# Turning two blocks of memory V by DMA, splitting the last copy and the first half of Wo in a two-part kernel on one core

## The chip, the cores and the metric

The kernel runs on one core of a Trainium2 chip. The metric is device time in microseconds (us) from one execution of the whole program; the runs of one kernel are summed up by their median. A profile of one execution adds, for each engine, when every instruction ran and what it waited for. The engines are named as the profile names them: PE (TensorE), DVE (VectorE), ACT (ScalarE), POOL (GpSimd) and SP (SyncE, which only issues DMAs).

## What is computed

Two independent models run on two inputs, and their outputs stand side by side in the last dimension. Part A is a diagonal state-space layer, part B attention with a recurrent memory of 8 rows in front of every segment of 32 tokens:

```python
def _A_ref(x, Lambda_re, Lambda_im, B_re, B_im, C_re, C_im, log_dt, Dskip):
    ...
    for t in range(L):
        h = Lam_bar[None, :] * h + Bu[:, t, :]
        hs.append(h)
    hseq = jnp.stack(hs, 1)
    y = 2.0 * jnp.einsum('blp,dp->bld', hseq, Cmat).real + x * Dskip[None, None, :]
    return y

def _B_ref(x, mem0, Wq, Wk, Wv, Wo, seg_len):
    ...
    mem = mem0
    for s in range(n_seg):
        xs = x[:, s * seg_len:(s + 1) * seg_len, :].copy()
        h = jnp.concatenate([mem, xs], axis=1)
        q = jnp.einsum('btd,dhe->bhte', h, Wq)
        k = jnp.einsum('btd,dhe->bhte', h, Wk)
        v = jnp.einsum('btd,dhe->bhte', h, Wv)
        scores = jnp.einsum('bhqe,bhke->bhqk', q, k) * scale
        scores = jnp.where(mask[None, None], scores, -1000000000.0)
        p = _softmax(scores, axis=-1)
        o = jnp.einsum('bhqk,bhke->bhqe', p, v)
        o = jnp.einsum('bhte,hed->btd', o, Wo)
        mem = o[:, :M, :].copy()
        outs.append(o[:, M:, :])
    return jnp.concatenate(outs, axis=1)
a = _A_ref(...)
b = _B_ref(...)
return jnp.concatenate([a, b], axis=-1)
```

Part A has 2048 tokens, width 1024 and 1024 complex states; part B has 2048 tokens in 64 segments, width 1024, 32 heads of 128, and 8 memory rows that each segment hands to the next. Inputs and outputs are bfloat16.

## The kernel before

**Stages.** The program is unrolled and runs in four stages.

1. Projections of V for all tokens of part B (`v_x`, in units of four tiles of 128 tokens for one of 8 head blocks of 4 heads) woven into part A's first stage (`stage1`: B products, then the scan). V rows go to DRAM, one tensor `b_vx` for each head block (`self.vx[hb]`). This stage ends at about 344 us.
2. Part A's output products (`stage2`): 16 tiles of 128 tokens, each in two halves of 512 columns, so 32 steps i = 0 to 31 of 16 matmuls. Between the steps stand pieces of part B: the values of the memory rows are first guessed (`og`, `guess`) and then, at i = 24 to 27, the memory's V rows of head blocks 0 and 1 are made by `v_mem`. This stage ends at about 467 us.
3. The q and k projections (`proj`) woven into attention (`attention`, `att_front`, `att_back`) by head pair, 16 pairs of 11 units. Before head pair hp, `load_v` brings its V from DRAM into the tile `b_v`: the padding of partitions 99 to 127 (for the first two pairs only), the rows of `b_vx`, and the rows of `b_vt`. Within this stage, at unit n = 12, the first half of the output weights is loaded into `wo0` (printed as tile `t` in the profile), and `v_mem` runs for head blocks 2 to 7.
4. The output products (`outproj_first`, `outproj`, `check`, `out_last`); the last tile's columns are done in pieces of 512, 256 and 256, so that little is left after the last matmul.

At the end a flag chooses a general path, which is not taken with these inputs.

**Memory V.** `v_mem` (L557) multiplies the memory columns of `b_xe` with a head block's `b_wv` into a PSUM tile `psP`, one row for each value column and 71 columns for the memory rows, and copies that to `b_vm` (L565). The rows are then wanted with memory rows on the partitions. Head blocks 0 and 1 turn them with four PE transposes each (L581) into another `psP`, copy to a staging tile `b_vst` on DVE (L583), and store from there with SP: one DMA to `b_vx` (L585) and three to `b_vt` (`store_t`, L555). Head blocks 2 to 7 turn them by DMA (L566 to L577): `b_vm` is cleared behind column 71, written to DRAM as `b_vmt`, read back by a transposing DMA into `b_vst`, and stored from there, all issued by SP. `v_mem` is a generator: each `yield` hands over to the next step of the loop around it.

**Order.** A scheduler orders each engine's instructions by when it takes them to be ready. PE and SP are held to the program's order in stage 1, SP also in stage 2; in stages 3 and 4 both are free, but for single instructions that are pinned behind all that was written before them on their engine (`keep_in_program_order`). Two of the three DMAs of `load_v` are pinned in this way: the padding and the rows of `b_vx`. A queue issues its DMAs strictly in its order, and one that waits holds up those behind it. The landing of DMAs from SP and ACT is told by eight semaphores, which the DMAs take in turn.

**The last piece.** `out_last` (L815) copies its three pieces with DVE, ACT, DVE (`k.copy("vsv"[i], ...)`, L823) and stores each with SP (L824). The three psP buffers and the one output tile `b_ost` are shared by the pieces.

**The queue of ACT in stage 2.** ACT issues the sixteen copies of `a_ot` (part A's output tile, two buffers) to DRAM (L345).

The loop around `v_mem` in stage 2 is at L1111 to L1129, the load of `wo0` at L1149.

## Time and profile before

| what | value |
|---|---|
| median of 3 runs | 1238.36 us (1238.14 to 1238.47) |
| profiled execution, whole / span | 1238.14 us / 1236.4 us |
| DMA, share of 16 engines over the span | q1 (SP) 48.4%, q10 (ACT) 6.1% |
| DMA moved | 174.20 MB, mean 141 GB/s |
| copies b_vm<-psP on DVE | 8, 455 ns each |
| copies b_vst<-psP on DVE in v_mem | 2, 410 ns each, the first at 445.9 us |
| transposing DMAs b_vst<-b_vmt on SP | 6, 565.6 to 901.1 us |
| load of wo0 (4096 KB) | issued at 510.35 us, 0.37 us of the queue |
| last copy b_ost<-psP on DVE | 128x256, 425 ns, at 1232.26 us |

The span runs from the first to the last instruction; the whole time has some 1.7 us around it. Busy time is the time in which an engine's instructions run; idle time in brackets stands before an instruction, with what ended it. "PEld" is the loading of weights, which overlaps PE. DMA issues stand at their queue's engine (SPq, ACTq), with the time that the issue took in the queue, not the time of the transfer.

### The profile page before, as it was taken

How to read it: one execution, taken by the hardware profiler on the slowest of the kernel's cores; microseconds unless marked ns; L12 is line 12 of the kernel's file. 1: busy time of each engine (PE TensorE's matmuls, PEld its weight loads, DVE VectorE, ACT ScalarE, POOL GpSimd, SP SyncE). 2: the span in 40 equal slices, each digit the busy share in tenths (PEclk: the TensorE clock that was granted, in tenths of full speed). 3: DMA queues.
4: the chain of work that ended last, by engine and by line, in shares of the span. 5: the costliest groups of instructions: out<-in, count | busy, mean ns of one | idle time of the engine just before them, and what ended most of it. 6: DMA issues, size and time to landing. Idle time of an engine off the chain costs nothing.

```text
span 1236.4 us, 19973 instructions
## 1 busy us (share of the span) xinstructions
PE 1226.7 (99%) x8104; PEld 655.0 (53%) x8174; DVE 680.7 (55%) x1270; ACT 266.6 (22%) x694; POOL 271.8 (22%) x437
## 2 busy tenths in 40 slices
PE   9999999999999999999999999999999999999998
PEld 4444444444455555556666656555665554445444
DVE  4799999998711124666666666666666641001000
ACT  4444444443310000211112211111221110000000
POOL 4111232112322321322222222323222320000000
PEclk9999999999999999999999999999999999999999
DMA  9943455562798834855464645546574279507000
GB/s 246 246 148 93 126 141 143 154 172 89 232 306 258 248 120 95 234 125 139 96 154 109 154 108 135 127 91 132 115 151 97 62 208 234 113 17 154 18 17 27
DMA packets 321268, 174.20 MB, mean 141 GB/s; under 512 B 145882, under 2 KB 308876, under 8 KB 321172
## 3 DMA queue, kind: packets, MB, share of 16 engines
q1 hardware_dynamic: 299076, 145.33, 48.4%
q10 hardware_dynamic: 21072, 24.38, 6.1%
q0 software_dynamic: 1024, 3.17, 0.7%
q8 instruction: 65, 1.06, 0.4%
q14 instruction: 31, 0.25, 0.1%
HBM read 84.42 MB, written 53.96 MB: 112 GB/s over the span
## 4 chain that ended last, share of the span: by engine, by line
PE 94%; DVE 4%; issue 1%; DMA 0%; ACT 0%; SPq 0%; DVEq 0%
PE psP L69 80%; PE psU L69 7%; PE psS L69 3%; PE psO L69 2%; PE psR L69 1%; DVE a_pr L284 1%; DVE a_pr L274 1%; DVE a_pr L279 1%; DMA b_xr<-in_B_x_dram 0%; DVE a_n L299 0%; DVE a_h L302 0%; DVE a_fr L232 0%; DVE a_tabh L243 0%; DVE a_tabh L240 0%; ACT a_g L285 0%
## 5 line engine op out<-in xcount | busy, mean ns | idle before, releaser
L69 PE MATMUL psP<-b_xe,b_wk 128*128 128x480 bf16 (+1 forms) x1280 | 247.5, 343 | 0.0
L69 PE MATMUL psP<-b_xe,b_wq 128*128 128x480 bf16 (+1 forms) x1280 | 247.5, 343 | 0.0
L69 PE MATMUL psP<-b_wv,b_xe 128*128 128x512 bf16 (+2 forms) x1027 | 223.0, 372 | 1.3 <-ACT b_xe L94 0.2
L689 POOL TENSOR_TENSOR b_m<-b_e,maskB 99x396 bf16<-99x396 bf16 (+1 forms) x160 | 134.7, 842 | 335.4 <-ACT b_e L688 335.4
L688 ACT ACTIVATE b_e<-psS 99x396 bf16<-99x396 f32 (+3 forms) x208 | 91.5, 442 | 530.4 <-PE psS L69 530.4
L69 PEld LDWEIGHTS <-b_wk 128*128 128x128 bf16 x1280 | 119.2, 98 | 94.2
L69 PEld LDWEIGHTS <-b_wq 128*128 128x128 bf16 x1280 | 118.5, 98 | 87.7
L69 PEld LDWEIGHTS <-b_xe 128*128 128x128 bf16 x1056 | 101.9, 98 | 119.1 <-ACT b_xe L94 0.4
L96 DVE CAST b_k<-psP 128x480 bf16<-128x480 f32 (+1 forms) x192 | 97.3, 528 | 100.0 <-PE psP L69 100.0
L96 DVE CAST b_q<-psP 128x480 bf16<-128x480 f32 (+1 forms) x192 | 97.3, 529 | 92.2 <-PE psP L69 90.9
L69 PEld LDWEIGHTS <-b_ol 128*128 128x128 bf16 x864 | 84.3, 98 | 94.4
L69 PE MATMUL psU<-a_xT,a_bt 128*128 128x512 bf16 x500 | 114.1, 379 | 0.6
L69 PE MATMUL psP<-t,a_hl 128*128 128x512 bf16 x497 | 112.3, 379 | 0.8
L96 DVE CAST b_ost<-psP 128x512 bf16<-128x512 f32 (+1 forms) x17 | 11.5, 676 | 177.6 <-PE psP L69 176.6
L69 PE MATMUL psP<-wo,b_ol 128*128 128x512 bf16 (+1 forms) x440 | 91.9, 364 | 0.4
L69 PE MATMUL psP<-t,b_ol 128*128 128x512 bf16 x408 | 91.7, 379 | 0.4
L94 ACT ACTIVATE b_vst<-psP 128x512 bf16<-128x512 f32 x126 | 72.5, 589 | 76.0 <-PE psP L69 69.9
L289 POOL TENSOR_SCALAR a_tt<-a_pr,a_tabf 128x1 f32<-128x1 f32 x48 | 34.7, 723 | 245.4 <-DVE a_pr L284 245.4
L706 DVE TENSOR_TENSOR b_ob<-psO,b_accR 99x384 bf16<-99x384 f32 x160 | 86.0, 554 | 2.9 <-DVE b_accR L705 0.4
L69 PEld LDWEIGHTS <-a_bt 128*128 128x128 bf16 x512 | 49.8, 98 | 59.5
L69 PEld LDWEIGHTS <-a_hl 128*128 128x128 bf16 x512 | 49.1, 98 | 56.7
L274 DVE TENSOR_TENSOR a_pr<-psU,a_tabf 128x2048 f32<-128x2048 f32 x32 | 73.1, 2283 | 9.2 <-PE psU L69 9.1
(203 smaller groups left out, 968.5 us busy)
## 6 DMA issues: line engine op xcount, KB each, us to landing
b_v<-b_vx SPq DMA_DIRECT2D x16, 1122.0 KB
b_wv<-in_B_Wv_dram SPq DMA_DIRECT2D x16, 1024.0 KB
b_vx<-b_vst ACTq DMA_DIRECT2D x24, 544.0 KB
b_on<-b_ob SPq DMA_DIRECT2D x15, 720.0 KB
a_hs<-a_h SPq DMA_DIRECT2D x32, 256.0 KB
b_wog<-in_B_Wo_dram SPq DMA_DIRECT2D x4, 2048.0 KB
b_wq<-in_B_Wq_dram SPq DMA_DIRECT2D x16, 512.0 KB
b_wk<-in_B_Wk_dram SPq DMA_DIRECT2D x16, 512.0 KB
```

The costliest lines, as they stand in the source:

```text
L69: r = f(*a, **kw)
L94: self.S.activation(out, in_, ACT.Copy)
L96: self.V.tensor_copy(out, in_)
L274: V.tensor_tensor(pr[:], u[:].unsqueeze(1).to_broadcast([128, 2, 2, TB]), view(t3, [[TB + 1, 2], [TB + 1, 2], [1, TB]]), ALU.mult)
L279: V.tensor_tensor(w, w, pr[:, :, 1, :], ALU.add)
L284: V.tensor_tensor_scan(w[:, j, :], rb, w[:, j, :], 0.0 if ini is None else ini[:, j:j + 1], ALU.mult, ALU.add)
L289: G.tensor_scalar(tt[:, j:j + 1], w[:, j, TB - 1:TB], t3[:, 1, TB:TB + 1], None, ALU.mult)
L688: k.S.activation(e[:, a:b, :, 0:n], s[0:GW, a:b, :, 0:n], ACT.Exp, scale=float(E) ** -0.5, accum_out=self.accE[0:GW, j:j + 1])
L689: k.G.tensor_tensor(mv[:, a:b, :, 0:n], e[:, a:b, :, 0:n], mask[0:GW, :, 0:n].unsqueeze(2).to_broadcast([GW, b - a, 2, n]), ALU.mult)
L706: V.tensor_tensor(self.ob[:, b0:b0 + n, :], o[0:GW, 0:n, 0:E], r.unsqueeze(2).to_broadcast([GW, n, E]), ALU.mult)
```

## The change

1. `v_mem` turns the rows of all head blocks by DMA; the PE transposes, their PSUM tile and the copy out of it are gone. For head blocks 0 and 1 the six DMAs (write of `b_vmt`, transpose, store to `b_vx`, three stores to `b_vt`) are issued by ACT, for the others by SP as before. `store_t` takes the queue as an argument.
2. In stage 2, `v_mem` of head block 1 starts at i = 27 in place of 26, and the generators are stepped at i = 24 to 29 in place of 24 to 27, three steps for each block in place of two.
3. The last output piece (256 columns) is copied by ACT (its last 128 columns) and DVE (its first 128).
4. The load of `wo0` (first 512 columns of Wo, all heads) is issued as two DMAs of 16 heads each.

```diff
-    def store_t(self, hb, s):
+    def store_t(self, hb, s, q):
...
-            self.k.SP.dma_start(self.vt[hb][r0:r0 + n, :].rearrange("n (h e) -> n h e", h=4), s[i:i + n, :, :])
+            q.dma_start(self.vt[hb][r0:r0 + n, :].rearrange("n (h e) -> n h e", h=4), s[i:i + n, :, :])
...
-        if hb > 1:
-
-            k.V.memset(vm[:, :, NM:128], 0.0)
-            k.SP.dma_start(self.vmt[hb][:], vm[:].rearrange("p h n -> p (h n)"))
-            yield
-            s = self.next_st()[:].rearrange("p i h e -> p (i h e)")[:, 0:576].rearrange("p (h e) -> p h e", h=4)
-            k.V.memset(s[:, :, E:EW], 1.0)
-            k.SP.dma_start_transpose(s[:, :, 0:E], self.vmt[hb][:])
-            yield
-            k.SP.dma_start(self.vx[hb][64:64 + NMX, :].rearrange("n (h e) -> n h e", h=4), s[0:NMX, :, 0:EW])
-            self.store_t(hb, s[:, :, 0:EW])
-            yield
+        q = k.SP if hb > 1 else k.nc.scalar
+        k.V.memset(vm[:, :, NM:128], 0.0)
+        q.dma_start(self.vmt[hb][:], vm[:].rearrange("p h n -> p (h n)"))
         yield
-        pt = k.ps("P", (128, 1024), BF16)
-        for h in range(4):
-            k.PE.transpose(pt[0:NM, h * 128:(h + 1) * 128], vm[:, h, 0:NM], k.ident[:])
-        st = self.next_st()
-        k.copy("v", st[0:NM, 0, :, 0:E], pt[0:NM, 0:512].rearrange("p (h e) -> p h e", h=4))
-        sv = st[:, 0, :, :].rearrange("p h e -> p (h e)")
-        k.SP.dma_start(self.vx[hb][64:64 + NMX, :], sv[0:NMX, :])
-        self.store_t(hb, st[:, 0, :, :])
+        s = self.next_st()[:].rearrange("p i h e -> p (i h e)")[:, 0:576].rearrange("p (h e) -> p h e", h=4)
+        k.V.memset(s[:, :, E:EW], 1.0)
+        q.dma_start_transpose(s[:, :, 0:E], self.vmt[hb][:])
+        yield
+        q.dma_start(self.vx[hb][64:64 + NMX, :].rearrange("n (h e) -> n h e", h=4), s[0:NMX, :, 0:EW])
+        self.store_t(hb, s[:, :, 0:EW], q)
         yield
...
-            k.copy("vsv"[i], ot[:, c0:c1], p[:, 0:c1 - c0])
+            if i < 2:
+                k.copy("vs"[i], ot[:, c0:c1], p[:, 0:c1 - c0])
+            else:
+                k.copy("s", ot[:, c0 + 128:c1], p[:, 128:c1 - c0])
+                k.copy("v", ot[:, c0:c0 + 128], p[:, 0:128])
...
-                if i in (24, 26):
-                    vm = b.v_mem((i - 24) // 2, wv[(i - 24) // 2])
-                if 24 <= i < 28:
+                if i in (24, 27):
+                    vm = b.v_mem((i - 24) // 3, wv[(i - 24) // 3])
+                if 24 <= i < 30:
                     next(vm)
...
-                k.SP.dma_start(wo0[:], b.Wo[:, :, 0:512])
+                for h in range(0, H, 16):
+                    k.SP.dma_start(wo0[:, h:h + 16, :], b.Wo[:, h:h + 16, 0:512])
```

## The prediction

> **What bounds the kernel.** I read the page's busy shares first, then the chain of waits, then the waits of TensorE alone, and after that the timeline around each place that the diff touches. Times in brackets below are us from the span's start.

> ```profile
> PE 1226.7 (99%) x8104; PEld 655.0 (53%) x8174; DVE 680.7 (55%) x1270; ACT 266.6 (22%) x694; POOL 271.8 (22%) x437
> ...
> PE 94%; DVE 4%; issue 1%; DMA 0%; ACT 0%; SPq 0%; DVEq 0%
> ```

> PE is busy in 99% of the span and makes 94% of the chain that ended last. A busy PE can hide gaps between pipelined matmuls, so its waits are read too, all of them:

> ```profile
> PE psR L69 <- DVE hpb L110: 1.3, 1, 1.3
> PE psU L69 <- DMA b_xr<-in_B_x_dram: 0.3, 1, 0.3
> PE psP L69 <- ACT b_xe L94: 0.2, 1, 0.2
> ```

> Three waits, 1.8 us, all in the first ten us. The starts of neighbouring matmuls say the same: 216 ns apart for 512 columns and 203 ns for 480, with the clock granted in full. From 1.28 to 1232 PE never stops. So time is won only where matmuls go away or the tail after the last one shrinks, and lost only where an operand now comes late or that tail grows.

> **Part 1: turning memory V of head blocks 0 and 1.** Removed from PE: 2 x 4 transposes.

> ```profile
> 445.07 0.39 PE L69 MATMUL psP<-ident,b_vm 128*71 128x128 bf16 x4
> 445.29 3.62 PE L69 MATMUL psP<-t,a_hl 128*128 128x512 bf16 x16
> ...
> 453.24 0.39 PE L69 MATMUL psP<-ident,b_vm 128*71 128x128 bf16 x4
> ```

> The columns are start, duration, engine, line, operation. The 0.39 is latency; what counts is the start of what follows: 445.29 - 445.07 = 0.22 us for four. Twice that is **-0.44 us** on the bounding engine. Lower bound 0 (if something else stops PE there), upper bound 2 x 0.39 = 0.78; I take 0.44, since starts are what a pipelined engine is paid in.

> VectorE loses two copies out of PSUM (0.41 each) and gains two clears of b_vm (0.25) and two of b_vst (0.09): 0.14 us less in all, under waits for PE of 2.5 to 3.8 us in each half tile of this stage. Two takings of the three psP buffers go as well. Neither moves the end.

> The work that comes in is a chain of DMAs that waits for itself. Head blocks 2 to 7 already run it on SP; head block 2 shows its price:

> ```profile
> 563.66 0.54 SPq L69 DMA_DIRECT2D b_vmt<-b_vm  x1
> ...
> 565.65 1.82 SPq L69 DMA_TRANSPOSE b_vst<-b_vmt  x1
> ...
> 570.76 0.98 SPq L69 DMA_DIRECT2D b_vx<-b_vst  x1
> 571.78 2.29 SPq L69 DMA_DIRECT2D b_vt<-b_vst  x3
> ```

> The transpose waits for the first write (2.0 us), the stores wait for the transpose (landed at 570.69, 5.0 after its issue), the last store is issued by 574.07 and its semaphore is full at 575.68: 10.4 us of queue, 12.0 us to landing. For block 0 the cast of b_vm ends at 442.28, the clear at 442.5, so issue ends at about 453 and everything has landed at 454.6; before, the stores were issued from 446.32 to 447.67. Block 1 begins one half tile later than before (i = 27 for 26): its matmuls end at 449.95 + 3.45 - 0.22 = 453.2, clear done at 453.9, issue over at 464.3, landed at 465.9.

> All of this stands in ScalarE's queue. What is queued behind it there?

> ```profile
> 483.34 0.29 ACT L688 ACTIVATE b_e<-psS 99x146 bf16<-99x146 f32 x1 [108.18 <-PE psS L69]
> ```

> The bracket is idle time: ScalarE computes nothing for 108 us, up to 483.34. It only issues the four last copies of a_ot to DRAM (445.99, 454.16, 461.29, 468.20 before). They go out 0.4, 0.3, 3 and 0 us later; a buffer of a_ot is written again 11 us after its copy was issued (tile 14 at 457.17, tile 15 at 464.08), and landing took 2 to 3.2 us. So the chain costs nothing on that engine; if it ran 19 us longer, the first exponentials would be late, and with them the scores' PSUM buffers. SP loses eight store issues (0.30 + 1.00 + 0.28 + 1.35 = 2.9 us) and POOL's queue is not touched; the load of Wv at 449.98 moves with block 1's matmuls to 453.2 and is used some 100 us later.

> [...] The rows above put the price of a turn on PE at 0.055 us and the DMA chain beside the path, and the sum goes by the rows.

> **Who waits for the late stores.** Head block 0's rows are read by the load of b_v for head pair 0. It is one slow piece (the padding of partitions 99 to 127) and the V rows behind it.

> ```profile
> 457.38 16.50 SPq L69 DMA_DIRECT2D b_v<-b_vx  x2
> ```

> ```profile
> 472.00:474.00 2.00, 2.00 (x12) 0.98 (x10) 1.38 (x5) 0.00 (x0) 0.00 (x0) 1.00 0.07 22
> ...
> 482.00:484.00 2.00, 2.00 (x15) 1.06 (x14) 0.88 (x2) 0.66 (x4) 0.13 (x1) 1.00 1.04 263
> 484.00:486.00 2.00, 2.00 (x15) 1.06 (x14) 0.66 (x1) 0.63 (x3) 0.87 (x3) 1.00 0.15 46
> ```

> ```profile
> 488.35 0.50 PE L69 MATMUL psO<-b_v,b_m 128*128 128x129 bf16 x6
> ```

> A window gives each engine's busy time, the clock, then DMA share and GB/s: while the padding drains only about one engine of sixteen works (22 GB/s), and the rows land at 483.87, the semaphore's last count. First use is at 488.35, so the slack is 4.5 us, 4.0 once PE runs 0.44 ahead. Block 0 has landed by 454.6, before the load's own start at 457.38: no stall, if nothing else holds that load.

> **Part 2: the last output piece.** Before, VectorE copies 256 columns in 0.42 (1232.26), then a store goes out at 1232.71 and lands at 1234.35, and the end follows. For 128 columns VectorE needs 425 - (692 - 425)/2 = 292 ns, ScalarE 384 - (597 - 384)/2 = 277 ns, from their rows at 512 and 256 columns. In parallel that saves 0.13. But both read one PSUM tile. The trace has one place where both engines read one:

> ```profile
> 1124.09 0.45 DVE L861 TENSOR_TENSOR c_df<-psP,b_gx 128x280 f32<-128x280 f32 x1 [3.31 <-PE psP L69]
> 1124.57 0.40 ACT L862 ACTIVATE c_sq<-psP 128x280 f32<-128x280 f32 x1 [10.80 <-DVE c_df L861]
> ```

> L862 reads nothing that L861 writes, and yet ScalarE waited for it: two readers were put in a row. So I take 277 + 40 (hand-over) + 292 = 609 ns for 425: **+0.18 us**, with -0.13 as the other bound. That row's readers took the same columns; the change's take different ones. [...]

> **Part 3: Wo in two pieces.** One more issue, 0.37 us as the row at 510.35 has it, on SP, which then stands still till 517.62. Same bytes, same queue; before, they landed at 524.38 and PE first reads them at 999.57. Cost 0; without that cover, 0.4.

> **Sum.** -0.44 + 0.18 = -0.26. The profiled execution took 1238.14 with a span of 1236.44 (1.7 around it): 1236.2 and 1237.9. The runs' median is 0.22 above it: **1238.1 us**.

> **Rivals.** (a) *The load of b_v comes late.* Its DMAs wait for more than their data: at 457.38 the wait ended as an a_ot copy landed (457.36), which shares one of eight completion semaphores, dealt out in turn, with the padding load. Four more DMAs now stand nearby, so it may draw one of block 1's chain. If that is the transpose (453.9 + 7.0 = 460.9), it is 3.5 late, inside the slack of 4.0. If it is the last store (465.9), it is 8.5 late and PE stalls 4.5: 1242.6. It decides from 461.4 on, and passes 0.2% from 464.1. For it: PE has no other slack this small and the padding sets the pace. Against: SP no longer has block 1's stores ahead of the load, so it can also start sooner. Chance 0.13, about even between little and much.
> (b) *The two copies run side by side*: 1238.36 - 0.44 - 0.13 = 1237.8. Against it stands the L862 row. Chance 0.07.
> (c) *The change doesn't do what it says to PE*: another wait eats the 0.44, leaving 1238.36 + 0.18 = 1238.5. Against it: PE waits for nothing else there. Chance 0.05.
> The forecast has the other 0.75.

> **How the numbers follow.** About 0.2% (2.5 us) is what a measurement of this kernel can tell from no change. A gain of that size would need 2.5 us of matmuls gone; the transposes are 0.44, the last copy as a whole 0.42: 0.03 for a cause that I don't see. Slower: half of (a), and 0.04 for stalls that I can't name, since instruction orders may be dealt anew: 0.11. Within: 0.86. The range begins at the bounds of both gains and the runs' spread, 1238.36 - 0.78 - 0.13 - 0.2, about 1237.2, and reaches to a stall of 2.2, half of (a)'s worst: 1240.3. The likeliest case alone: 1237.6 to 1238.6.

> **What would show it.** Right: no matmul on b_vm; PE waits still 1.8 us; the first matmul on b_v about 0.4 sooner; in the tail ScalarE's 128 columns, then VectorE's, waiting for it. Wrong: a PE wait that ends with a DMA of b_v near 488; copies that overlap; exponentials that start after 484 behind a DMA issue.

## The result and the profile after

The changed kernel takes 1244.68 us (median; 1244.40 to 1246.41) against 1238.30 for the kernel before on the same chip: a ratio of **1.0054 [1.0037, 1.0072]**. It is 6.4 us slower; 1238.1 had been forecast, with a range up to 1240.3. The profiled execution has a span of 1242.7 us, 6.3 more than before.

First the busy shares of the changed kernel, with the chain that ended last under them:

```profile
PE 1228.6 (99%) x8096; PEld 655.1 (53%) x8166; DVE 679.8 (55%) x1272; ACT 266.7 (21%) x695; POOL 271.8 (22%) x437
...
PE 92%; DVE 4%; DMA 2%; issue 1%; ACTq 0%; ACT 0%; SPq 0%; DVEq 0%
```

Eight PE instructions are gone, as the diff says, and PE is still busy for 99%. But DMA, 0% of the chain before, is now 2%. A share that new is worth a search: somewhere the end waits for transfers. TensorE's waits (what is waited for; then total, times, longest, in us) say where:

```profile
PE psP L69 <- DVE a_ot L343: 4.3, 2, 3.6
PE psR L69 <- DVE hpb L110: 1.3, 1, 1.3
PE psU L69 <- DMA b_xr<-in_B_x_dram: 0.5, 1, 0.5
PE psP L69 <- DMA b_xe<-in_B_x_dram: 0.3, 1, 0.3
PE psP L69 <- ACT b_xe L94: 0.2, 1, 0.2
```

The first line is new. PE waits twice for a free psP buffer, and the one that should free it is VectorE's add into a_ot, in stage 2. VectorE is only 55% busy, so the question is what VectorE waits for. Its timeline in that stretch (start, duration, operation, and in brackets the idle time before it and what ended it):

```profile
448.34 0.25 DVE L567 MEMSET b_vm<- 128x228 bf16 x1 [5.62 <-DMA b_vmt<-b_vm]
448.50 1.41 DVE L343 TENSOR_TENSOR a_ot<-psP,a_xd 128x512 bf16<-128x512 f32 x2
459.89 0.09 DVE L571 MEMSET b_vst<- 128x32 bf16 x1 [9.98 <-DMA b_vt<-b_vst]
459.90 0.69 DVE L343 TENSOR_TENSOR a_ot<-psP,a_xd 128x512 bf16<-128x512 f32 x1
...
464.45 0.25 DVE L567 MEMSET b_vm<- 128x228 bf16 x1 [3.50 <-DMA b_vmt<-b_vm]
...
474.13 0.09 DVE L571 MEMSET b_vst<- 128x32 bf16 x1 [7.46 <-DMA b_vt<-b_vst]
```

Four small clears, 0.09 to 0.25 us each, stand in VectorE's queue **ahead of** the adds, with 26.6 us of idle time before them in all. Not all of it costs: while VectorE waits, PE can still fill the free psP buffers. The waits of 5.62 and 3.50 us stop PE nowhere, the one of 7.46 us stops it for 0.75 us, the one of 9.98 us for 3.56 us; by the last two the buffers cover some 6.4 to 6.7 us. None of the clears belongs to the block being turned at the time. The clear at 448.34 is that of b_vm for block 1: there is one b_vm buffer, and block 0 is still being written out of it. The one at 459.89 clears the staging buffer for head block 2, work that is due some 100 us later; it waits for block 0's stores to leave that buffer. The two at 464.45 and 474.13 are the same pair, one block on. The scheduler orders by when it takes an instruction to be ready, and it took these to be ready before the transfers had landed. In the kernel before, three of them stood at about the same place, and the same timeline shows them without a bracket:

```profile
449.65 0.09 DVE L572 MEMSET b_vst<- 128x32 bf16 x1
454.45 0.25 DVE L568 MEMSET b_vm<- 128x228 bf16 x1
457.82 0.09 DVE L572 MEMSET b_vst<- 128x32 bf16 x1
```

They cost nothing there: no write to DRAM read b_vm, and the stores had landed (the last of block 0 at 448.99, of block 1 at 457.56). How the stop looks on TensorE:

```profile
453.45 3.62 PE L69 MATMUL psP<-t,a_hl 128*128 128x512 bf16 x15
460.63 12.21 PE L69 MATMUL psP<-t,a_hl 128*128 128x512 bf16 x47 [3.56 <-DVE a_ot L343]
...
474.96 1.53 PE L69 MATMUL psP<-b_xe,b_wk 128*128 128x199 bf16 x16 [0.75 <-DVE a_ot L343]
```

The windows (each engine's busy time, granted clock, DMA share, GB/s) show what came on top. After the first stop the clock falls: at half from 461.20 on, for 3.41 us.

```profile
456.00:460.00 4.00, 1.07 (x5) 0.39 (x4) 0.10 (x2) 0.00 (x0) 0.00 (x0) 1.00 0.75 244
461.00:465.00 4.00, 4.00 (x13) 1.50 (x11) 0.55 (x2) 0.00 (x0) 3.86 (x6) 0.57 0.31 109
466.00:470.00 4.00, 4.00 (x19) 1.85 (x19) 0.67 (x1) 0.00 (x0) 0.00 (x0) 1.00 0.12 27
```

Thirteen matmuls of 512 columns in 4 us at a clock of 0.57, nineteen at full clock: about 3.41 / 2 = 1.7 us lost while PE counts as 100% busy.

And the first window has a DMA share of 0.75 at 244 GB/s: the little chain does not have the transfers to itself. The chain of waits through this stretch (start, duration, what) prices it:

```profile
442.75 5.42 DMA b_vmt<-b_vm
...
448.19 2.77 DMA b_vst<-b_vmt
...
453.93 5.80 DMA b_vt<-b_vst
...
461.00 3.28 DMA b_vmt<-b_vm
```

The write of b_vm was priced at 2.0 us to landing and takes 5.4. The last store was priced at 1.6 us from the end of its issue, which is 2.5 from its start, and takes 5.8 from its start. Beside them, in SP's queue, go two loads of Wv (1 MB each, for head blocks 2 and 3), which the scheduler also issues early, at 442.25 and 453.65:

```profile
442.25 11.78 SPq L69 DMA_DIRECT2D b_wv<-in_B_Wv_dram  x2
```

Each load goes out just ahead of one of the two slow steps, and the step lands with it: the write, issued 0.50 us behind the first load, at 448.17 (the load at 448.37), and the last store, 0.28 us behind the second, at 459.74 (the load at 459.42).

**The sum, by the starts of matmuls** (after minus before). Ahead of the change, at the matmuls on b_wv in stage 2, +0.45: 441.02 against 440.57, from the first loads of the program. To the half tile that starts at 453.45 against 453.46: -0.46, the transposes. From there to the first matmul on b_wq, 19.23 us against 13.81: +5.42, the first stop (3.72 by starts) and the half clock (1.7). To the first on b_wk, 2.28 against 1.38: +0.90, the second stop. Together +6.31, and the first scores start at 489.29 against 482.98, 6.31 later. Another 0.19 comes at 506, where the last of three matmuls on b_v waits for POOL's b_m, too short a wait for the list. The last matmul starts 6.50 later. From there to the end the changed kernel needs 4.27 us, the kernel before 4.50, of which the last section tells.

### The profile page after: what moved, and what is told of

The parts are those of the page before. It is cut to its first block, busy times and chain, and to the rows that moved or that the text cites. A ratio compares the mean times of both kernels' runs of the same rounds, so it can differ in the third digit from the quotient of the medians.

```text
span 1242.7 us, 19967 instructions
## 1 busy us (share of the span) xinstructions
PE 1228.6 (99%) x8096; PEld 655.1 (53%) x8166; DVE 679.8 (55%) x1272; ACT 266.7 (21%) x695; POOL 271.8 (22%) x437
## 3 DMA queue, kind: packets, MB, share of 16 engines
q8 instruction: 65, 1.06, 0.4%
## 4 chain that ended last, share of the span: by engine, by line
PE 92%; DVE 4%; DMA 2%; issue 1%; ACTq 0%; ACT 0%; SPq 0%; DVEq 0%
PE psP L69 78%; PE psU L69 7%; PE psS L69 3%; PE psO L69 2%; PE psR L69 1%; DVE a_pr L284 1%; DVE a_pr L274 1%; DMA b_vt<-b_vst 1%; DMA b_vmt<-b_vm 1%; DVE a_pr L279 1%; DMA b_vst<-b_vmt 0%; DMA b_xr<-in_B_x_dram 0%; DVE a_n L299 0%; ACTq L555 0%; ACTq L574 0%
## 5 line engine op out<-in xcount | busy, mean ns | idle before, releaser
L69 PE MATMUL psP<-b_xe,b_wk 128*128 128x480 bf16 (+1 forms) x1280 | 247.5, 343 | 0.7 <-DVE a_ot L343 0.7
L69 PE MATMUL psP<-b_xe,b_wq 128*128 128x480 bf16 (+1 forms) x1280 | 247.5, 343 | 0.0
L69 PE MATMUL psP<-b_wv,b_xe 128*128 128x512 bf16 (+2 forms) x1027 | 223.1, 373 | 1.5 <-DMA b_xe<-in_B_x_dram 0.3
L69 PEld LDWEIGHTS <-b_wk 128*128 128x128 bf16 x1280 | 119.2, 98 | 95.1 <-issue 0.9
L69 PEld LDWEIGHTS <-b_xe 128*128 128x128 bf16 x1056 | 101.9, 98 | 119.4 <-ACT b_xe L94 0.3
L69 PEld LDWEIGHTS <-b_wq 128*128 128x128 bf16 x1280 | 118.5, 98 | 87.7
L69 PEld LDWEIGHTS <-b_ol 128*128 128x128 bf16 x864 | 84.3, 98 | 94.4
L69 PE MATMUL psP<-t,a_hl 128*128 128x512 bf16 x497 | 113.9, 383 | 4.3 <-DVE a_ot L343 3.6
L69 PE MATMUL psU<-a_xT,a_bt 128*128 128x512 bf16 x500 | 114.1, 379 | 0.6
L69 PE MATMUL psP<-wo,b_ol 128*128 128x512 bf16 (+1 forms) x440 | 91.9, 364 | 0.4
L69 PE MATMUL psP<-t,b_ol 128*128 128x512 bf16 x408 | 91.7, 379 | 0.4
L94 ACT ACTIVATE b_vst<-psP 128x512 bf16<-128x512 f32 x126 | 72.3, 589 | 76.7 <-PE psP L69 69.6
L69 PEld LDWEIGHTS <-a_hl 128*128 128x128 bf16 x512 | 49.6, 99 | 62.1 <-issue 6.2
L69 PEld LDWEIGHTS <-a_bt 128*128 128x128 bf16 x512 | 49.8, 98 | 59.4
```

The source lines that it names most:

```text
L69: r = f(*a, **kw)
L94: self.S.activation(out, in_, ACT.Copy)
```

## The experiments

Two theories for the first batch. **Clears**: the early clears hold VectorE, so pinning them in the written order removes the loss. **Queue or load**: the loss is the chain itself, above all the load of b_v that it delays (rival (a) of the prediction); pinning the clears then only moves the stop.

**e1_pin_clears**: the changed kernel, with both clears of v_mem kept where they are written.

```diff
-        k.V.memset(vm[:, :, NM:128], 0.0)
+        k.tc.keep_in_program_order(k.V.memset(vm[:, :, NM:128], 0.0))
...
-        k.V.memset(s[:, :, E:EW], 1.0)
+        k.tc.keep_in_program_order(k.V.memset(s[:, :, E:EW], 1.0))
```

> The changed kernel, in which the clears of b_vm and b_vst on VectorE are pinned at their place in the program, so that the clears of head blocks 2 and 3 no longer stand in stage 2 ahead of the adds on a_ot. Theory 1 (clears that wait for a DMA landing hold up VectorE's queue, so PSUM buffers stay full and TensorE stops for 3.6 + 0.7 us, and the granted clock halves for 3.4 us): both stops and the half clock go away; 1238.36 - 0.44 + 0.18 = 1238.1 us, up to 1239 if the load of b_v, whose padding waits for block 1's transpose, is now the late one near 488 us. Rival (the late load of b_v, or the DMA chain in ScalarE's queue, is what costs): still above 1242.

Measured: 1243.45 (1241.65 to 1243.72), 1.0041 [1.0028, 1.0055]: of the first theory the waits came true, the time did not. VectorE's clears now wait for nothing, and PE's waits for a_ot are gone. But the first line of its waits is a new one, and the timelines show its place and the load that it waits for:

```profile
PE psO L69 <- DMA b_v<-b_vx: 3.5, 1, 3.5
PE psR L69 <- DVE hpb L110: 1.3, 1, 1.3
PE psU L69 <- DMA b_xr<-in_B_x_dram: 0.9, 1, 0.9
```

```profile
491.83 0.50 PE L69 MATMUL psO<-b_v,b_m 128*128 128x129 bf16 x6 [3.45 <-DMA b_v<-b_vx]
```

```profile
464.52 17.06 SPq L69 DMA_DIRECT2D b_v<-b_vx  x2
```

That is rival (a). The padding load of b_v is issued at 464.52, 0.02 us after block 1's transpose, which has the same completion semaphore, has landed (464.50); it had been 457.38 before. That is 7.1 late against a slack of 4.0, which gives 3.1; 3.45 was measured. The changed kernel has this lateness too (466.91) and doesn't show it, because there PE had already been held up for longer. Both theories are half right: the two stops lie one behind the other, and taking the first away uncovers the second. The profiled execution is the one of 1241.65, with the clock in full (1.00) after the stop; the other four, 1243.45 to 1243.72, are 1.8 to 2.1 longer, and their mean granted clock on record is 0.998 to 0.999 against 1.000, which fits one half clock of 3.41 us. Those were not traced.

**e2_v_alone**: the changed kernel with the old last copy and the single load of Wo, so only the turning of memory V is left.

```diff
-            if i < 2:
-                k.copy("vs"[i], ot[:, c0:c1], p[:, 0:c1 - c0])
-            else:
-                k.copy("s", ot[:, c0 + 128:c1], p[:, 128:c1 - c0])
-                k.copy("v", ot[:, c0:c0 + 128], p[:, 0:128])
+            k.copy("vsv"[i], ot[:, c0:c1], p[:, 0:c1 - c0])
...
-                for h in range(0, H, 16):
-                    k.SP.dma_start(wo0[:, h:h + 16, :], b.Wo[:, h:h + 16, 0:512])
+                k.SP.dma_start(wo0[:], b.Wo[:, :, 0:512])
```

> Only memory V by DMA; the last copy and the load of Wo as before the change. Theory 1: nearly the whole loss is here, 1244.68 - 0.18 = 1244.5 us, with a stop of TensorE of 3 to 4 us near 457 us and the clock at half behind it. Rival (the load of Wo in two pieces or the split copy costs, for instance by another order of the DMA semaphores): below 1241.

Measured: 1244.95 (1244.5 to 1247.7), 1.0058 [1.0044, 1.0072]. The whole loss is in this part:

```profile
PE psP L69 <- DVE a_ot L343: 3.5, 2, 3.3
```

Here the half clock lasts 6.83 us, from 459.29, of which PE is back for 5.8 from 460.36 on: 2.9 lost.

**e3_copy_alone**: the kernel before with the split last copy, which is the reverse of the first hunk above.

> The kernel before with the last 256 columns copied by two engines. If the two readers of one PSUM tile go one behind the other: the last store is issued 0.18 us later after the last matmul than before, 1238.5 us. If they go side by side: 0.13 earlier, 1238.2 us. Both are inside 0.2% of before.

Measured: 1239.35 (1238.70 to 1239.83), 1.0007 [0.9998, 1.0016]. The copies stand in a row, as the L862 row had said, and the last store is issued 0.94 us after the last matmul's start against 0.76: +0.18 as forecast. The time, though, is +0.9. The interval still touches no change, but all eleven runs lie above all 21 of the kernel before. In the traced execution the rest is at the end: one of the store's sixteen landings comes 2.30 us after the issue, the others 1.62 at the latest. See e11.

**e4_wo_alone**: the kernel before with the load of Wo in two pieces, the reverse of the second hunk.

> The kernel before with the first half of Wo loaded in two pieces. Theory 1: no wait of TensorE anywhere, 1238.3 us. Rival (it moves a wait of the DMA queue into attention): TensorE waits between 510 and 600 us, above 1239.

Measured: 1238.32 (1238.08 to 1238.73), 0.9999 [0.9990, 1.0008]; no wait of PE. The cost of 0 holds.

For the second batch the question was why the chain takes so long. **Shared engines**: the two Wv loads slow every step of it; issue them later and both stops go, with or without pinned clears. **The chain as such**: it is too long beside this stage; then late loads change little, and only moving block 1 away helps.

**e5_pin_clears_late_wv**: e1, with the two Wv loads pinned to the fourth unit of the attention.

```diff
+        r = (e or self.k.SP).dma_start(w[:, :, c0:c1], self.Wf[2][:, :, hb * 512 + c0:hb * 512 + c1])
+        if self.late:
+            self.k.tc.keep_in_program_order(r)
...
+            if n == 3:
+                b.late = True
+                wpre = {h: b.load_wv(h) for h in (2, 3)}
+                b.late = False
...
-                    vm = b.v_mem(hp // 2 + 1)
+                    vm = b.v_mem(hp // 2 + 1, wpre.pop(hp // 2 + 1, None))
```

> Pinned clears as in the first experiment, and the two 1 MB loads of Wv for head blocks 2 and 3, which ran in the middle of the two DMA chains, are issued in attention (unit 3) instead. Theory 1 as it stands now (the chains are long because each runs beside a 1 MB load: first write 5.4 us to landing in place of 2.0; the padding of b_v waits for block 1's transpose by way of its completion semaphore): the padding starts near 459 in place of 464.5, the rows of b_v land near 485.5, ahead of their use at 488, TensorE doesn't wait there; 1238.46 - 0.44 + 0.18 = 1238.2 us, at most 1238.8. Rival (the chain is long by itself, so that b_v stays late): a wait near 488 of 2 us or more, 1241 to 1243.5 us.

Measured: 1237.75 (1237.50 to 1237.93), 0.9994 [0.9985, 1.0003]. No wait of PE from stage 2 to the first scores. The write of b_vm lands in 1.7 us, not 5.4; the padding goes out at 459.67, 4.9 us earlier than in e1, its rows land at 486.45, and the first matmul on b_v starts at 488.36. Block 0's chain takes 10.0 us (443.00 to 453.04) in place of 17.0.

**e6_late_wv**: the late Wv loads alone, the clears left free.

> The changed kernel with the two loads of Wv moved to attention and the clears left where the scheduler put them. Theory 1: block 0's stores land near 454 in place of 459.7, so VectorE is held only 1 to 3 us ahead of its adds, which three PSUM buffers cover; no stop of TensorE over 0.5 us, no half clock, 1238.2 us, at most 1239. Rival (the clears ahead of the adds cost by themselves, whatever the length of the chain): a stop of 2 us or more near 457, above 1241 us.

Measured: 1237.76 (1237.43 to 1238.59), 0.9995 [0.9986, 1.0004], the same as e5. This is the run that settles it, because the clears stand ahead of the adds here too, and the first three even wait for the same transfers:

```profile
444.85 0.25 DVE L569 MEMSET b_vm<- 128x228 bf16 x1 [1.91 <-DMA b_vmt<-b_vm]
453.16 0.09 DVE L573 MEMSET b_vst<- 128x32 bf16 x1 [3.02 <-DMA b_vt<-b_vst]
458.02 0.25 DVE L569 MEMSET b_vm<- 128x228 bf16 x1 [3.69 <-DMA b_vmt<-b_vm]
...
467.75 0.09 DVE L573 MEMSET b_vst<- 128x32 bf16 x1 [6.26 <-PE psP L69]
```

```profile
PE psR L69 <- DVE hpb L110: 1.3, 1, 1.3
PE psP L69 <- DMA b_wv<-in_B_Wv_dram: 0.5, 1, 0.5
PE psU L69 <- DMA b_xr<-in_B_x_dram: 0.4, 1, 0.4
PE psP L69 <- ACT b_xe L94: 0.2, 1, 0.2
```

What held VectorE for 10.0 us at 459.89 now holds it for 3.0, up to 453.16, and the longest wait, 6.26 us at the last clear, is still one that the three psP buffers cover. (The trace puts its end down to PE; block 1's last store had landed 0.1 us before, at 467.63.) Block 0's chain takes 10.0 us (442.97 to 452.93). The padding of b_v still goes out 0.02 us after block 1's transpose has landed, now at 460.59, 3.2 later than before and inside the slack of 4.0. So the misplaced clears are the way by which the loss reaches PE first; the length of the chain decides whether there is one. Not every step is slower beside the loads: block 0's transpose takes 2.7 us here and 2.8 in the changed kernel.

**e7_block1_later**: clears pinned, block 0 as in the change, block 1 turned on SP in the attention of head pair 0; old last copy, single load of Wo.

```diff
-        q = k.SP if hb > 1 else k.nc.scalar
+        q = k.SP if hb else k.nc.scalar
...
-                if i in (24, 27):
-                    vm = b.v_mem((i - 24) // 3, wv[(i - 24) // 3])
-                if 24 <= i < 30:
+                if i == 24:
+                    vm = b.v_mem(0, wv[0])
+                if 24 <= i < 27:
...
-            if hp % 2 == 0 and 2 < hp + 2 < HP:
+            if hp % 2 == 0 and hp + 2 < HP:
...
+                    vm = b.v_mem(hp // 2 + 1, wv[1] if hp == 0 else None)
```

> Memory V of head block 0 by DMA from ScalarE in stage 2, that of head block 1 in attention of head pair 0 by DMA from SP as the later blocks; clears pinned; last copy and load of Wo as before the change. Theory 1: no block 1 chain is left that the padding of b_v can wait for, no clears stand ahead of the adds, TensorE has eight transposes less: 1238.46 - 0.44 = 1238.0 us. Rival (a chain anywhere near the load of b_v makes it late, or block 1's V comes late for head pair 2): a wait of TensorE in 480 to 620 us, above 1239.5.

Measured: 1237.81 (1237.62 to 1238.08), 0.9995 [0.9985, 1.0004]. With no second chain near it, the padding goes out at 457.35 as in the kernel before (457.38), although block 0's own write of b_vm still took over 5 us beside a Wv load (issued 443.29, transpose at 448.60). With the clears pinned, one stretched step is hidden here; two chains in a row (e1) are not.

**e8_pin_clears_sp**: e1 with the whole chain on SP's queue.

```diff
-        q = k.SP if hb > 1 else k.nc.scalar
+        q = k.SP
```

> Pinned clears, and the DMAs of head blocks 0 and 1 issued by SP in place of ScalarE. Theory 1 (the length of the chain and what stands behind it decide, not ScalarE's queue): the pinned padding of b_v now also stands behind all of block 1's stores in SP's queue, so it starts later than 464.5 and TensorE's wait near 488 grows from 3.5 to 5 us or more: 1245 us or above. Rival (issuing from ScalarE is the fault): the wait shrinks, below 1240 us.

Measured: 1246.47 (1246.31 to 1247.31), 1.0067 [1.0051, 1.0082], the worst of all. SP's queue shows why: the padding load (last line) goes out at 467.91, behind the second block's transpose and stores (461.23 to 467.35), where e1 had it at 464.52.

```profile
461.23 1.26 SPq L69 DMA_TRANSPOSE b_vst<-b_vmt  x1
...
465.06 2.29 SPq L69 DMA_DIRECT2D b_vt<-b_vst  x3
...
467.91 16.45 SPq L69 DMA_DIRECT2D b_v<-b_vx  x2
```

```profile
494.45 0.81 PE L69 MATMUL psO<-b_v,b_m 128*128 128x129 bf16 x6 [6.26 <-DMA b_v<-b_vx]
```

PE stops for 6.26 us, and the half clock from 491.12 to 497.95 costs half of the 3.5 us after the stop. 6.26 + 1.75 - 0.44 + 0.18 = 7.75, and from the last store's issue to the end it takes 0.20 more than before (3.93 against 3.73): 7.95, against a measured +8.07. ScalarE's queue is thus the better one of the two: it saved SP the eight issues, as the prediction had counted them.

The third batch asked what is left to win, and what the split copy really costs.

**e9_late_wv_plain_tail**: e5 with the old last copy and the single load of Wo.

> Memory V by DMA for head blocks 0 and 1, clears pinned, loads of Wv for blocks 2 and 3 in attention, last copy and load of Wo as before the change. The same kernel with the split copy and Wo in two gave 1237.75. If the split copy costs what the handing over from one reader to the other takes: 0.18 less, and 0.1 more for a last store on an earlier one of the eight semaphores, 1237.65 us. If the split copy costs more than that in most executions (the kernel before with it alone gave +0.9): 1237.2 us or less.

Measured: 1237.69 (1237.52 to 1237.82), 0.9993 [0.9984, 1.0002]. Against e5 (1237.75) the split copy is worth less than 0.1 in this kernel. This is the fastest version found, 0.78 us below the kernel before by the medians; the interval still touches no change, but all eleven runs lie below all 21 of the kernel before. Not all of it is the merit of the turning by DMA: the way from the last store's issue to the end is 0.35 shorter than before (3.38 against 3.73, last section), and with the transposes' 0.44 that makes 0.79. In the profile only the waits at the head of the program are left:

```profile
PE psR L69 <- DVE hpb L110: 1.3, 1, 1.3
PE psU L69 <- DMA b_xr<-in_B_x_dram: 1.1, 1, 1.1
```

**e10_two_psum_tiles**: e9 with the last piece as two matmul groups of 128 columns in two PSUM tiles, so that the two engines need not wait for one another.

```diff
-        for i, (c0, c1) in enumerate(((0, 512), (512, 768), (768, 1024))):
+        for i, (c0, c1) in enumerate(((0, 512), (512, 768), (768, 896), (896, 1024))):
...
-            k.copy("vsv"[i], ot[:, c0:c1], p[:, 0:c1 - c0])
+            k.copy("vssv"[i], ot[:, c0:c1], p[:, 0:c1 - c0])
```

> The kernel of the line above with the last 256 columns made in two PSUM tiles of 128 columns, the first copied by ScalarE while TensorE makes the second, the second by VectorE. The last copy takes 292 in place of 425 ns and waits for no other reader: 0.13 less than the line above, if 128-column matmuls start 56 ns apart as the transposes did. Rival (matmuls of 128 columns are held by their weight loads, 98 ns each): 64 x 42 ns = 2.7 us more.

Measured: 1238.34 (1238.12 to 1238.75), 0.9999 [0.9990, 1.0008]: 0.65 above e9 where 0.13 less was expected. The mechanism works, as the timeline shows: ScalarE's copy is over long before VectorE's.

```profile
1230.53 0.28 ACT L94 ACTIVATE b_ost<-psP 128x128 bf16<-128x128 f32 x1 [1.35 <-PE psP L69]
...
1232.31 0.29 DVE L96 CAST b_ost<-psP 128x128 bf16<-128x128 f32 x1 [6.32 <-PE psP L69]
```

Matmuls of 128 columns start 56 ns apart, those of 256 columns 109 (before), so halving the piece costs PE 0.1 us at most, and the store goes out 0.57 us after the last matmul, 0.19 sooner. But in the traced execution, the slowest of the eleven, one of its sixteen landings takes 2.69 us, the others 1.45 at the most; an instruction fetch of 16 KB starts 0.23 us after the store's issue and takes 1.44.

**e11_copy_alone_again**: e3 once more, for its last landing.

> The kernel before with the split copy, once more, for a second look at its end. Theory (one of the sixteen DMA engines is late for the last store because the code behind ScalarE's branch is fetched at the same moment): the last of the sixteen landings again 0.6 to 0.7 us behind the others, while fetches start at 1.0 us after the store's issue. Rival (chance of one execution): all land within 0.3 us and the span is 1236.8 us or less.

Measured, one run: 1239.42. The last landing comes after 2.63 us, 1.0 behind the others (1.62 at the latest) where 0.6 to 0.7 had been expected, and an instruction fetch starts 1.02 us after the store's issue. The late landing stands in all three traces where the fetch starts 1.01 to 1.03 us after the issue (e3, e8, e11). Where it starts at +1.36 or later (before, e2, e4, e7, e9) there is none, and at +1.08 to +1.10 (the changed kernel, e1, e5, e6) there is none either. A difference of 0.05 us is a thin line, so that the fetch delays the store is not shown; it wasn't tried by moving the fetch alone.

## Why the prediction was wrong

Two terms of Part 1 failed. The first decides whether there is a loss, the second where it comes out.

**The term that was mis-sized** is the chain: 12.0 us from the first write's issue to the last landing, "its price" taken from head block 2. Measured: 442.75 to 459.74, 17.0 us. Block 2's stretch was not a quiet one: from 564 to 568 the DMA engines moved 215 GB/s, from 568 to 572 293. Loads of Wq and Wk (512 KB each) went out at 564.30 and 564.83, and block 2's transpose, issued 0.82 us behind the second, landed 0.5 us after it and took 5.0 us (2.7 in e6). But its write and its last store had no such load just ahead of them. In the changed kernel these two steps have one, 0.50 and 0.28 us ahead, of 1 MB each. The prediction had the second of these loads in view, and moved it to 453.2 asking only when its data is used. e6, which moves only the two loads, brings block 0's chain back to 10.0 us and the loss to nothing; that is shown. That a step waits behind the load in front of it is read from the landings alone.

**The term put at nothing**: "VectorE loses two copies out of PSUM (0.41 each) and gains two clears of b_vm (0.25) and two of b_vst (0.09): 0.14 us less in all", and, of this and the psP takings, "Neither moves the end." The clears were costed by how long they run. What they wait for was not asked, nor which other clears use the same buffers. b_vm and the staging buffers had become sources of a slow DMA chain, and the clears for the *next* users, blocks 1, 2 and 3, stood in VectorE's queue ahead of the adds. Three of them stand in the trace of before already, at 449.65, 454.45 and 457.82, in the very stretch that the prediction looked at. Weighed against the chain's priced landing (454.6 for block 0) they would have been seen to wait some 5 us, which the psP buffers cover; with the measured length the wait is 10 us and PE stops.

Even with the clears out of the way, the long chain costs 5.0 us (e1). At that length rival (a), in the case where the padding shares the transpose's semaphore, would have been the forecast.

**Rival (a)** had the right mechanism, a shared completion semaphore that ties the padding load to block 1's transpose, and the right place. It put that landing at 460.9, inside the slack; in e1 it was 464.5 and the stop followed within 0.4 us of the slack's account. In the changed kernel itself it is hidden behind the earlier stop. It was also priced by the stop's length alone. TensorE's half clock after a stop added 1.7 us in the changed kernel and 2.9 in e2, which no row of before could show, since it had no stop and a mean clock of 1.000. With the loads moved away (e6) the transpose lands at 460.57, near the 460.9 of the prediction, and PE doesn't wait, as it had said for that case.

Two readings of the prediction were off without an effect. The copies of a_ot took up to 4.8 us to land, not 3.2, and in the changed kernel they go out 3.6 to 8.9 us later, not 0.4 to 3; no add waits for one. The load of wo0 had landed at 525.86, not 524.38.

**What held.** The transposes were worth 0.44 (0.46 by starts), and in e5, e6, e7 and e9 kernels with the turned memory V are 0.6 to 0.8 us below the one before, if their intervals are taken by the middle. ScalarE's queue was free for the chain, and e8 shows SP's was not. The split copy's engines stand in a row, although they take different columns, +0.18 to the store's issue, in e3 and in the changed kernel (ScalarE's copy ends at 1239.04, VectorE's starts at 1239.07):

```profile
1238.76 0.28 ACT L94 ACTIVATE b_ost<-psP 128x128 bf16<-128x128 f32 x1 [3.06 <-PE psP L69]
1239.07 0.29 DVE L96 CAST b_ost<-psP 128x128 bf16<-128x128 f32 x1 [6.55 <-ACT b_ost L94]
```

Wo in two pieces cost nothing (e4). So Part 3 was priced right, and Part 2 as far as the store's issue; what the split copy costs in time differs, +0.9 alone (e3) and under 0.1 in e5 against e9. The forecast of 1238.1 is within 0.4 us of what the change does once the two Wv loads are out of its way (e6: 1237.76). The tail accounts for that much: from the last store's issue to the end e6 takes 3.31 us against 3.73, a term that the forecast didn't have.

## What to carry to other kernels

When a buffer becomes the source of a DMA, look for every later instruction that writes that buffer, find where the scheduler has put it, and read what stands behind it in its engine's queue: the clear of 0.09 us at 459.89 held an idle engine for 9.98. The price of a short chain of dependent transfers did not carry over from another stretch (12.0 us for head block 2, 17.0 for block 0, 10.0 for block 0 in e6): look which large loads will be issued just ahead of each of its steps. Moving two of them was worth more than the change here: 6.9 us (1244.68 to 1237.76 in e6) against a forecast of 0.26. And when an experiment removes one stop and the time hardly moves, read the waits again before giving the theory up: a second stop may have been hidden behind the first, as the one of 3.45 us in e1 was.

## What the runs showed of the hardware

**The end of the program went with the place of the last store's semaphore.** At the end SP waits for eight completion semaphores one after another, some 0.08 us each (the first seven of the changed kernel at 1240.30 to 1240.78). In the kernel before, the third of these waits ends with the landing of the last store (1234.35, the wait at 1234.37), and the eighth comes at 1234.73; in the changed kernel the store's own is the eighth (landed at 1240.99, the wait at 1241.01). From the last store's issue to the end, where no landing is late, it takes 3.73 us if that store has the third in the row (before), 3.62 for the fourth (e4), 3.37 to 3.47 for the seventh (e2, e7, e9) and 3.31 to 3.40 for the last (the changed kernel, e1, e5, e6). The changed kernel's tail is 0.23 shorter than before in spite of the slower copy for this reason: 0.18 lost, 0.40 won by the order in which semaphores were dealt out. Such 0.4 us are no merit of an edit to the tail, and hide one as easily.
